# A fused attention and SwiGLU kernel: two weight loads ahead of a transposed load, an offset for every operation in the order, and warm-up on a constant

## The chip, the cores and the metric

The kernel runs on one core of a Trainium2 chip. The time is that of one execution on the device in microseconds (us); three runs of the kernel before gave 235.48, 235.54 and 235.83 us, so the median is 235.54 us.

A core has four compute engines that run side by side, each working through its own instructions in the order in which the program lists them: TensorE (PE in the profile, with its weight loads as PEld), VectorE (DVE), ScalarE (ACT) and GpSimd (POOL). SyncE (SP) issues most of the DMA transfers; its queue is SPq. An instruction that waits holds up everything behind it on its engine.

## The reference

The inputs are bfloat16: x is 2048 x 512, wqkv 512 x 1536, wo 512 x 512, w1 and w3 512 x 1376, w2 1376 x 512, gate_w has 512 entries.

```python
qkv = x @ wqkv                      # 32 heads of 16
scores = q @ k.T * 16 ** -0.5       # per head
mask = (i - j >= 0) & (i - j < 256) # causal, a window of 256 keys
a = softmax(where(mask, scores, -1e9)) @ v   # then heads joined, @ wo
b = (silu(x @ w1) * (x @ w3)) @ w2
g = sigmoid((x * gate_w).sum(-1))
out = g * a + (1 - g) * b
```

B_x is not used: both halves read A_x.

## The kernel before

**Layout.** x is held transposed in SBUF as `xT`, in four quarters of 512 tokens, called x0 to x3 here. x0 is loaded plainly and turned by TensorE (L383). x1, x2 and x3 are turned by the DMA, four transfers of 128 columns each (`turn_x`, issued by SP at L289). Attention goes by four chunks `c` of 128 columns (8 heads) and 16 key blocks `t` of 128 tokens. The SwiGLU half goes by four token blocks `tcb` of 512 and eleven column tiles `f` of 128, the last of them of 96 columns.

**Work on TensorE.** K and Q projections (L443), four matmuls of 512 columns each per chunk and quarter; V (L496), for two chunks at once; scores of a key block, 8 matmuls on 32-row strips (L551), and of the block edges, 32 small ones (L601); probabilities times V (`pv`, L691), in two halves per chunk and quarter, on 17-column strips; w1 and w3 (L841), the leftover columns (L778), w2 (L894), wo (L923) and the last tile's w2 in three parts (L950). The program calls the three shapes "full", "row" (L551, L601) and "column" (L691).

**Other engines.** ACT does the exponentials (L555, L605, 1.88 us each), half of the copies of K and the tanh of the SwiGLU half. POOL masks the exponentials (L560, L565, L618), rearranges V (L532) and copies the last columns of w1 and w3 into `wA` and `wB` (L754). DVE evacuates most of PSUM. Scores have one PSUM buffer of four banks (`su`), everything else has four of one bank (`ch`).

**The order.** `opening()` issues the first loads in a fixed order. Everything else is an `Op` handed to `Plan.add` with an engine, a duration, dependencies and a due time. `Plan.emit` is a list scheduler that runs in Python when the program is built: again and again it takes the engine that can start first, and on it, among the operations that can start at that moment, the one with the smallest due time, ties by number (`rank`). The result is a fixed order of instructions for each engine; on the chip they wait only for semaphores. The scheduler's idea of when a load has landed is a table, `landed`, in us.

Two constants in `rank` act on the shapes: while TensorE is in a shape other than full, row and column operations get due times smaller by `ADJ`; while it is in full shape, column operations get `SEP` added, which is negative. An exponential may be held back for up to `HOLD` ahead of other work on ACT.

**Numbers of operations.** Each `Op` has a running number, `len(self.ops)` at its creation. Number 17 is POOL's small write that gates x3: `late(25.8, ...)` makes an entry that ends at 25.8 us, a two-element memset on POOL with due time 25.8 that depends on it (L358), and four `turn_x` operations on SP behind it. The program thus uses POOL's place in its order to hold SP back. The rest of wqkv is gated in the same way near 67 us.

**SP's opening order.** x0's first half, K's weights (one half, the other by ACT), Q's weights, w1 and w3 columns 0:256, V's weights, x1 (four), w1 and w3 columns 256:768, x2 (one), w1 columns 768:1376, x2 (one), w3 columns 768:1376, x2 (two). Below, "first", "second" and "third columns" mean 0:256, 256:768 and 768:1376.

**Warm-up.** 25 matmuls on a tile `warm`, which DVE sets to zero (L312), run on TensorE from the start; two more stand before the first projection.

Of the kernel before, what the change touches and what calls it, by code (L numbers as in the profile page):

```python
# [8 lines left out]
ACT = mybir.ActivationFunctionType  # L9
BF16 = mybir.dt.bfloat16  # L10
# [5 lines left out]
P = 128  # L16
KB = 64
BIG = 3.0e38
SLACK = 0.04


PIPE = {"DVE": 0.105, "ACT": 0.112, "POOL": 0.045}
LAT = {"PE": 0.205}
# [23 lines left out]
class Plan:  # L47
# [7 lines left out]
    def add(self, eng, dur, fn, deps=(), due=0.0, take=(), free=(), lat=None, form="full", port=False):  # L55
        if lat is None:
            lat = LAT.get(eng, 0.05)
        op = Op(eng, dur, fn, deps, due, list(take), list(free), lat, len(self.ops), form, port)
        self.ops.append(op)
        return op  # L60
# [91 lines left out]
def kernel(  # L152
# [12 lines left out]
    nc = tc.nc  # L165
# [19 lines left out]
    SCALE = float(DH) ** -0.5  # L185
    WARM = 25

# [4 lines left out]
    xs = pp.tile([P, 4, D], BF16, name="xs")  # L192
    warm = pp.tile([P, P], BF16, name="warm")
    wqkv_sb = pp.tile([P, NDC, 3 * D], BF16, name="wqkv_sb")
# [38 lines left out]

    K = {"T0": 3.834, "TA": 174.183, "TF0": -2.174, "TF1": 214.702, "PV": -18.741, "EDGE": -2.057, "HOLD": -5.699, "LEAD": -2.792, "QLEAD": -4.754, "V": 6.656, "O0": 12.623, "O1": 1.536, "O2": 8.341, "O3": 35.5, "FE": 0.655, "PE": 7.925, "VE": -2.0, "MK": 33.193, "UP": 8.561, "_km": 1.0, "_lo": 1.0, "LE": 0.445, "ADJ": 6.464, "SEP": -25.111, "BE": 6.303, "OE": 5.748, "END": 6.616}
    plan = Plan({"su": 1, "ch": 4, "Em": len(Em), "Ee": len(Ee), "tt": 2, "h1": 2,
# [71 lines left out]
    def warm_up(n):  # L307
        for i in range(n):
            nc.tensor.matmul(su[:, 0, 0:P], lhsT=warm[:], rhs=warm[:], start=True, stop=True)

    def opening():
        nc.vector.memset(warm[:], 0.0)  # L312
        constants()
        warm_up(WARM)

        nc.scalar.activation(out=gt[:, 0:4], in_=warm[:, 0:4], func=ACT.Tanh)
        load_x(0, 2, nc.sync)
# [6 lines left out]
        load_w(wqkv_sb, A_wqkv, 2 * D, 2 * D + 2 * P)  # L324
        turn_x(1)
        load_w(w1_sb, B_w1, 2 * P, 6 * P)
        load_w(w3_sb, B_w3, 2 * P, 6 * P)
        turn_x(2, 0, 1)
        load_w(w1_sb, B_w1, 6 * P, F)
        turn_x(2, 1, 2)  # L330
        load_w(w3_sb, B_w3, 6 * P, F)
        turn_x(2, 2, 4)
# [9 lines left out]
    step = TA / (NDC * NT)  # L342
    landed = {"x": [3.75, 3.75, 4.45, 4.45, 12.2, 21.5], "w13": [7.2, 8.1, 15.4, 18.7],
              "qkv": [5.25, 6.2, 8.8], "gw": 8.0}

# [23 lines left out]

    x_in.append(late(25.8, xT[0:1, 0, 3 * 512:3 * 512 + 2], [lambda c=c: turn_x(3, c, c + 1) for c in range(NDC)], 1.27, 2.5))  # L370
    for b, us in ((1, 66.5), (0, 68.5), (2, 70.5)):
# [208 lines left out]
    def edge_batch(c, h):  # L580
# [56 lines left out]
        if K["_lo"]:  # L637
            edge_ready[(c, h)] = [add("POOL", 1.2, lambda lo=lo: low(lo), [x], due) for lo in (0, KB)]
            edge_ready[(c, h)].append(add("DVE", 0.45 if not last else 0.6, high, [x], due - K["MK"], port=True))
        else:  # L640
            edge_ready[(c, h)] = [add("DVE", 0.84, lambda half=half: mask(half), [x], due - K["MK"], port=True) for half in range(2)]
# [109 lines left out]
    for dst, c0, src in ((wA, 0, w1_sb[:, :, F0:F0 + FA]), (wA, FA, w3_sb[:, :, F0:F0 + FA]),  # L751
# [3 lines left out]

        w_ab.append(add("POOL", 0.4, w_copy, [w13_in[3]], 22.0))

# [6 lines left out]
    for tcb in range(NTC):  # L764
# [66 lines left out]
        for f in range(NFC):  # L831
# [33 lines left out]
            win = [w13_in[0 if f < 2 else 2 if f < 6 else 3]]  # L865
            win3 = [w13_in[1]] if f < 2 else []
            a = plan.pieces(HALF, 0.2155, lambda lo, hi, half=half, job=job: half(job, w1_sb, lo, hi),
# [134 lines left out]
```

## Time and profile before

| | |
|---|---|
| median of three runs | 235.54 us |
| the profiled execution | 236.38 us |
| its span, first to last instruction | 234.7 us |
| TensorE busy | 225.7 us (96%) |
| ScalarE busy | 182.8 us (78%) |
| VectorE busy | 179.5 us (77%) |
| GpSimd busy | 153.6 us (65%) |
| SP queue, share of the 16 DMA engines | 18.1% |

The profile is of one execution, whose own time is 236.38 us; 1.7 us of that lie outside the span. Matmuls are pipelined, so a group of matmuls overlaps the next one's start by some 0.16 us, and starts, not ends, tell the pace. A few per cent of the matmul records are missing. A timeline merges equal instructions: "x8" with a start and a duration is eight of them. The chain of waits is followed back from the last instruction; a line in it is a piece that held up the end.

### The profile page before, as it was taken

How to read it: one execution, taken by the hardware profiler on the slowest of the kernel's cores; microseconds unless marked ns; L12 is line 12 of the kernel's file. 1: busy time of each engine (PE TensorE's matmuls, PEld its weight loads, DVE VectorE, ACT ScalarE, POOL GpSimd, SP SyncE). 2: the span in 40 equal slices, each digit the busy share in tenths (PEclk: the TensorE clock that was granted, in tenths of full speed). 3: DMA queues.
4: the chain of work that ended last, by engine and by line, in shares of the span. 5: the costliest groups of instructions: out<-in, count | busy, mean ns of one | idle time of the engine just before them, and what ended most of it. 6: DMA issues, size and time to landing. Idle time of an engine off the chain costs nothing.

```text
span 234.7 us, 8251 instructions
## 1 busy us (share of the span) xinstructions
PE 225.7 (96%) x3590; PEld 116.1 (49%) x3626; DVE 179.5 (77%) x318; ACT 182.8 (78%) x165; POOL 153.6 (65%) x245
## 2 busy tenths in 40 slices
PE   8899999999999999999999999999999999999995
PEld 7454644555454444446464556435444445445553
DVE  5455985973789897988297988969498978869675
ACT  3488998976779899887889999988778997887310
POOL 7164979579765986565668768697669855474500
PEclk9999999999999999999999999999999999999999
DMA  6999034600004000000000002200000002120102
GB/s 191 193 210 291 4 45 108 189 20 1 3 19 120 3 8 17 3 3 3 0 4 3 3 4 62 53 3 4 0 3 3 3 6 56 58 91 6 67 25 89
DMA packets 20652, 11.57 MB, mean 49 GB/s; under 512 B 10024, under 2 KB 20616, under 8 KB 20616
## 3 DMA queue, kind: packets, MB, share of 16 engines
q1 hardware_dynamic: 19920, 10.62, 18.1%
q8 instruction: 28, 0.46, 0.9%
q10 hardware_dynamic: 696, 0.43, 0.6%
q14 instruction: 8, 0.07, 0.1%
HBM read 6.85 MB, written 2.10 MB: 38 GB/s over the span
## 4 chain that ended last, share of the span: by engine, by line
PE 80%; SPq 6%; DMA 6%; POOL 4%; issue 2%; DVE 1%
PE ch L841 26%; PE ch L894 15%; PE ch L443 10%; PE ch L691 8%; PE su L551 7%; PE ch L923 6%; SPq L289 5%; PE ch L496 4%; DMA wqkv_sb<-in_A_wqkv_dram 2%; DMA w_sb<-in_B_w_dram 2%; PE su L601 2%; SPq L296 1%; DMA xT<-in_A_x_dram 1%; POOL Ee L618 1%; PE ch L950 1%
## 5 line engine op out<-in xcount | busy, mean ns | idle before, releaser
L555 ACT ACTIVATE Em<-su 128x2048 bf16<-128x2048 f32 x60 | 112.6, 1877 | 24.8 <-PE su L551 20.8
L841 PE MATMUL ch<-xT,w_sb 128*128 128x512 bf16 x301 | 76.3, 380 | 1.6 <-issue 0.8
L560 POOL TENSOR_SCALAR_AFFINE_SELECT Em<-Em 64x512 bf16<-64x512 bf16 x60 | 43.4, 724 | 36.5 <-ACT Em L555 35.6
L618 POOL TENSOR_SCALAR_AFFINE_SELECT Ee<-Ee 64x1024 bf16<-64x1024 bf16 x32 | 37.6, 1174 | 16.3 <-ACT Ee L605 15.0
L841 PEld LDWEIGHTS <-w_sb 128*128 128x128 bf16 x320 | 28.4, 98 | 34.4 <-issue 4.9
L565 POOL TENSOR_SCALAR_AFFINE_SELECT Em<-Em 64x512 bf16<-64x512 bf16 x56 | 37.3, 667 | 3.3
L855 DVE SCALAR_TENSOR_TENSOR h<-tt,ch 128x512 bf16<-128x512 bf16 (+1 forms) x44 | 29.8, 678 | 11.1 <-ACT tt L851 10.7
L894 PE MATMUL ch<-w_sb,hT 128*128 128x512 bf16 x141 | 36.1, 380 | 1.0 <-issue 0.8
L443 PE MATMUL ch<-xT,wqkv_sb 128*128 128x512 bf16 (+1 forms) x131 | 34.1, 369 | 1.8 <-DMA wqkv_sb<-in_A_wqkv_dram 0.9
L532 POOL COPY vs<-vs 64x256 bf16<-64x256 bf16 x64 | 28.9, 452 | 7.3 <-DVE vs L520 2.7
L605 ACT ACTIVATE Ee<-su 128x2048 bf16<-128x2048 f32 x16 | 30.0, 1878 | 4.2 <-PE su L601 3.1
L861 DVE SCALAR_TENSOR_TENSOR hT<-h,ch 128x512 bf16<-128x512 bf16 x40 | 27.2, 679 | 2.5 <-PE ch L841 1.0
L851 ACT ACTIVATE tt<-ch 128x512 bf16<-128x512 f32 (+1 forms) x44 | 26.2, 595 | 1.3 <-PE ch L841 1.1
L691 PEld LDWEIGHTS <-vs 128*17 128x17 bf16 x1664 | 20.6, 92 | 6.2 <-issue 4.6
L691 PE MATMUL ch<-Em,vs 128*17 128x256 bf16 (+2 forms) x672 | 22.7, 242 | 0.1
L691 PE MATMUL ch<-Ee,vs 128*17 128x64 bf16 x992 | 22.3, 193 | 0.0
L894 PEld LDWEIGHTS <-hT 128*128 128x128 bf16 x150 | 13.5, 98 | 16.2 <-issue 2.7
L898 DVE TENSOR_SCALAR bsb<-ch,omg 128x512 bf16<-128x512 f32 x15 | 11.0, 738 | 11.6 <-PE ch L894 11.4
L443 PEld LDWEIGHTS <-wqkv_sb 128*128 128x128 bf16 x136 | 12.4, 99 | 14.2 <-issue 2.1
L551 PE MATMUL su<-qT,kz 32*128 32x256 bf16 x240 | 17.3, 278 | 0.1
L496 PE MATMUL ch<-wqkv_sb,xT 128*128 128x256 bf16 x128 | 16.7, 273 | 0.2 <-DVE tn L715 0.2
L551 PE MATMUL su<-qT,k 32*128 32x256 bf16 x240 | 16.7, 268 | 0.0
(84 smaller groups left out, 245.9 us busy)
## 6 DMA issues: line engine op xcount, KB each, us to landing
out_dram<-ot SPq DMA_DIRECT2D x15, 128.0 KB, 1.7
wqkv_sb<-in_A_wqkv_dram SPq DMA_DIRECT2D x5, 256.0 KB, 4.9
w_sb<-in_B_w_dram SPq DMA_DIRECT2D x2, 608.0 KB, 5.5
w_sb<-in_B_w_dram SPq DMA_DIRECT2D x3, 384.0 KB, 3.8
w_sb<-in_B_w_dram SPq DMA_DIRECT2D x2, 512.0 KB, 5.2
w_sb<-in_B_w_dram SPq DMA_DIRECT2D x2, 256.0 KB, 6.3
wo_sb<-in_A_wo_dram SPq DMA_DIRECT2D x4, 128.0 KB, 2.3
xs<-in_A_x_dram SPq DMA_DIRECT2D x1, 256.0 KB, 2.8
```

Of the source, the lines that this page charges most:

```text
L443: nc.tensor.matmul(pst[:, t0:t1], lhsT=wqkv_sb[:, dc, col + c * P:col + (c + 1) * P], rhs=xT[:, dc, tq * 512 + t0:tq * 512 + t1], start=(d ...
L532: nc.gpsimd.tensor_copy(out=v_of(to, base, a), in_=v_of(half, 0, a))
L551: nc.tensor.matmul(su[:, s, a * 256:(a + 1) * 256], lhsT=head_keys(r, t, a), rhs=qT[r, q0:q0 + 256], start=True, stop=True)
L555: nc.scalar.activation(out=Em[job.at["Em"]][:], in_=su[:].rearrange("p s (a q) -> p s a q", a=2), func=ACT.Exp, scale=SCALE)
L560: nc.gpsimd.affine_select(out=e, in_=e, pattern=[[0, 8], [1, KB]], compare_op=ALU.is_ge, fill=0.0, base=0, channel_multiplier=-1)
L565: nc.gpsimd.affine_select(out=e, in_=e, pattern=[[0, 8], [-1, KB]], compare_op=ALU.is_ge, fill=0.0, base=-1, channel_multiplier=1)
L605: nc.scalar.activation(out=Ee[ej.at["Ee"]][:].rearrange("p s t k q -> p s (t k q)"), in_=su[:], func=ACT.Exp, scale=SCALE)
L618: nc.gpsimd.affine_select(out=e, in_=e, pattern=[[0, 4], [0, 4], [1, KB]], compare_op=ALU.is_ge, fill=0.0, base=0, channel_multiplier=-1)
L691: nc.tensor.matmul(po[32 * s:32 * s + VW, lo - 512 * w:hi - 512 * w], lhsT=vs[:, i, a * VW:(a + 1) * VW], rhs=mov, start=(n == 0), stop=(n ...
L841: nc.tensor.matmul(ch[job.at["ch"]][:], lhsT=wA[:, dc, :] if joint else w[:, dc, f * P:(f + 1) * P], rhs=xT[:, dc, tcb * 512:(tcb + 1) * 512],
L855: nc.vector.scalar_tensor_tensor(out=h1[job.at["h1"]][ru, :], in0=tt[job.at["tt"]][rg, :], scalar=1.0, in1=ch[job.at["ch"]][rg, :], op0=AL ...
L894: nc.tensor.matmul(bps[:], lhsT=ht[:, mm * P:(mm + 1) * P], rhs=w2_sb[0:fs, f, :], start=(f == 0), stop=(f == NFC - 1))
```

## The change

- In `opening()`, the second columns of w1 and w3 are issued ahead of x1, the third columns of w1 ahead of x2, and those of w3 after the first of x2's four transfers.
- `landed` has new times. Up to now w1's and w3's second columns had one entry for both, and so had their third columns; now each load has its own.
- The gate of x3 is entered at 20.5 us, not 25.8.
- `Plan.add` adds `SHIFT[n]` to the due time of operation n. The list has 1520 numbers with a spread (standard deviation) of 15.2. Number 17 is 16.41.
- The constants in `K` are new, among them the spacing of the attention's due times (`TA`), `ADJ` and `SEP`; some durations in the scheduler's tables differ.
- The warm-up is 26 matmuls on a constant of ones that the program has anyway; the tile `warm` and its memset go.

```diff
+SHIFT = [
+    0, 0, 0, 0, 0, 0, 0, 0, 0, 0, 0, 0, 0, 0, 0, 0, 0, 16.41, 17.18, -1.15, 9.76, -3.89, -4.94, -3.98, -10.53, 6.23,
...
+    7.93, 89.38, 4.39, -2.31, 9.54, 0, 105.24, -33.46, -30.49, -22.75, -41.96,
+]
-PIPE = {"DVE": 0.105, "ACT": 0.112, "POOL": 0.045}
+PIPE = {"DVE": 0.105, "ACT": 0.112, "POOL": 0.0}
@@ def add
-        op = Op(eng, dur, fn, deps, due, list(take), list(free), lat, len(self.ops), form, port)
+        n = len(self.ops)
+        due += SHIFT[n] if n < len(SHIFT) else 0.0
+        op = Op(eng, dur, fn, deps, due, list(take), list(free), lat, n, form, port)
@@
-    WARM = 25
+    WARM = 26
-    warm = pp.tile([P, P], BF16, name="warm")
-    K = {"T0": 3.834, "TA": 174.183, "TF0": -2.174, "TF1": 214.702, "PV": -18.741, "EDGE": -2.057, "HOLD": -5.699, "LEAD": -2.792, "QLEAD": -4.754, "V": 6.656, "O0": 12.623, "O1": 1.536, "O2": 8.341, "O3": 35.5, "FE": 0.655, "PE": 7.925, "VE": -2.0, "MK": 33.193, "UP": 8.561, "_km": 1.0, "_lo": 1.0, "LE": 0.445, "ADJ": 6.464, "SEP": -25.111, "BE": 6.303, "OE": 5.748, "END": 6.616}
+    K = {"T0": 3.896, "TA": 206.496, "TF0": 0.258, "TF1": 224.823, "PV": -10.571, "EDGE": -3.579, "HOLD": -5.698, "LEAD": -3.708, "QLEAD": -6.04, "V": 10.539, "O0": 15.639, "O1": -7.5, "O2": 2.592, "O3": 31.747, "FE": 1.561, "PE": 14.011, "VE": -7.01, "MK": 68.425, "UP": 9.802, "_km": 1.0, "_lo": 1.0, "LE": -2.888, "ADJ": 16.608, "SEP": -51.372, "BE": 8.744, "OE": 1.749, "END": 5.976}
@@ def warm_up
-            nc.tensor.matmul(su[:, 0, 0:P], lhsT=warm[:], rhs=warm[:], start=True, stop=True)
+            ones = nc.const_aps.tensor_like(1.0, ident[:])
+            nc.tensor.matmul(su[:, 0, 0:P], lhsT=ones, rhs=ones, start=True, stop=True)
@@ def opening
-        nc.vector.memset(warm[:], 0.0)
-        nc.scalar.activation(out=gt[:, 0:4], in_=warm[:, 0:4], func=ACT.Tanh)
+        nc.scalar.activation(out=gt[:, 0:4], in_=nc.const_aps.tensor_like(1.0, gt[:, 0:4]), func=ACT.Tanh)
         load_w(wqkv_sb, A_wqkv, 2 * D, 2 * D + 2 * P)
-        turn_x(1)
         load_w(w1_sb, B_w1, 2 * P, 6 * P)
         load_w(w3_sb, B_w3, 2 * P, 6 * P)
+        turn_x(1)
+        load_w(w1_sb, B_w1, 6 * P, F)
         turn_x(2, 0, 1)
-        load_w(w1_sb, B_w1, 6 * P, F)
+        load_w(w3_sb, B_w3, 6 * P, F)
         turn_x(2, 1, 2)
-        load_w(w3_sb, B_w3, 6 * P, F)
         turn_x(2, 2, 4)
@@
-    landed = {"x": [3.75, 3.75, 4.45, 4.45, 12.2, 21.5], "w13": [7.2, 8.1, 15.4, 18.7],
-              "qkv": [5.25, 6.2, 8.8], "gw": 8.0}
+    landed = {"x": [3.6, 3.6, 4.4, 4.4, 14.5, 20.6], "w13": [7.45, 8.3, 10.8, 16.6, 12.2, 18.8],
+              "qkv": [5.25, 6.5, 9.0], "gw": 8.0}
@@
-    x_in.append(late(25.8, xT[0:1, 0, 3 * 512:3 * 512 + 2], [lambda c=c: turn_x(3, c, c + 1) for c in range(NDC)], 1.27, 2.5))
+    x_in.append(late(20.5, xT[0:1, 0, 3 * 512:3 * 512 + 2], [lambda c=c: turn_x(3, c, c + 1) for c in range(NDC)], 1.27, 2.5))
@@ def edge_batch
-            edge_ready[(c, h)] = [add("POOL", 1.2, lambda lo=lo: low(lo), [x], due) for lo in (0, KB)]
-            edge_ready[(c, h)].append(add("DVE", 0.45 if not last else 0.6, high, [x], due - K["MK"], port=True))
+            edge_ready[(c, h)] = [add("POOL", 1.15, lambda lo=lo: low(lo), [x], due) for lo in (0, KB)]
+            edge_ready[(c, h)].append(add("DVE", 0.6, high, [x], due - K["MK"], port=True))
@@
-        w_ab.append(add("POOL", 0.4, w_copy, [w13_in[3]], 22.0))
+        w_ab.append(add("POOL", 0.4, w_copy, [w13_in[5]], 22.0))
@@
-            win3 = [w13_in[1]] if f < 2 else []
+            win3 = [w13_in[1 if f < 2 else 4 if f < 6 else 5]]
```

86 rows, old and new, of the table SHIFT are left out of this document.

## The prediction

> **What bounds the kernel now.** First the page's busy times and its chain that ended last, then TensorE's waits, then the timeline of TensorE at the places of those waits, then the chain for the start.
>
> ```profile
> PE 225.7 (96%) x3590; PEld 116.1 (49%) x3626; DVE 179.5 (77%) x318; ACT 182.8 (78%) x165; POOL 153.6 (65%) x245
> PE 80%; SPq 6%; DMA 6%; POOL 4%; issue 2%; DVE 1%
> ```
>
> TensorE is the bound: no other engine is above 78%, and the chain runs on it for 80% of the span. From its waits:
>
> ```profile
> PE ch L443 <- DMA wqkv_sb<-in_A_wqkv_dram: 0.9, 1, 0.9
> PE ch L443 <- DMA xT<-in_A_x_dram: 0.4, 1, 0.4
> ```
>
> Two waits for loads; all other rows of that view are 0.2 us pieces. Those are missing records: TensorE has 36 gaps of 0.21 to 0.23 us, one matmul of 512 columns long, and the groups lack 36 such records (w1/w3 316 of 336, w2 156 of 165, projections 115 of 120, wo 62 of 64). What is left are two places, in TensorE's timeline:
>
> ```profile
> 17.70 0.38 PE L443 MATMUL ch<-xT,wqkv_sb 128*128 128x512 bf16 x1
> 18.20 0.82 PE L841 MATMUL ch<-xT,w_sb 128*128 128x512 bf16 x3
> ...
> 37.45 0.81 PE L443 MATMUL ch<-xT,wqkv_sb 128*128 128x512 bf16 x3
> 38.62 0.38 PE L443 MATMUL ch<-xT,wqkv_sb 128*128 128x512 bf16 x1 [0.36 <-DMA xT<-in_A_x_dram]
> ...
> 73.78 1.46 PE L841 MATMUL ch<-xT,w_sb 128*128 128x512 bf16 x6
> 75.17 0.29 PE L551 MATMUL su<-qT,kz 32*128 32x256 bf16 x4
> 75.29 0.28 PE L551 MATMUL su<-qT,k 32*128 32x256 bf16 x4
> 75.50 1.25 PE L841 MATMUL ch<-xT,w_sb 128*128 128x512 bf16 x5
> ```
>
> Starts of 512-column matmuls stand 0.2155 us apart. From 17.70 to 18.20 is 0.28 too long: w3's second columns, for which the weight load at 18.19 waits. From 37.45 three matmuls reach to 38.10, the fourth starts at 38.62: 0.52 us for x3. The last four lines show a change of shape: six matmuls from 73.78 end at 75.07 and the row starts at 75.17, 0.10 later; its second half starts at 75.29, streams 0.11 and is followed at 75.50, again 0.10 later. **From 8.8 us to the last matmul TensorE thus stands still for 0.80 us in all; the rest is matmuls and changes of shape.** The start, in the chain that ended last:
>
> ```profile
> 1.83 5.85 DMA wqkv_sb<-in_A_wqkv_dram
> 7.70 1.16 SPq L289
> 8.90 1.26 SPq L289
> 10.21 1.26 SPq L289
> ...
> 17.11 5.54 DMA w_sb<-in_B_w_dram
> 22.70 0.40 POOL wA L754
> ...
> 31.43 0.10 POOL xT L358
> 31.55 1.12 SPq L289
> ...
> 35.88 2.70 DMA xT<-in_A_x_dram
> 38.62 0.38 PE ch L443
> ```
>
> The second transfer of x1 was issued 0.02 us after Q's weights had landed (7.68), with which it has nothing to do: the second DMA behind V's load waits for the one that carried Q, whatever it loads. And x3 is late because POOL waited until 22.70 for w3's third columns, then worked without a pause and came to the gate at 31.43, planned for 25.8 or later.
>
> **The change, part by part.** The sum is made against the profiled execution, 236.38 us, span 234.7; the median of 235.54 is 0.84 lower. The profiled execution has a wait of 1.0 us for Q's weights (K's eight matmuls start 0.11 apart to 6.57, Q's start at 7.73). I take that to be most of the 0.84 and subtract the changes from both alike.
>
> *Second columns first.* w1's takes the place of x1's first transfer (issued at 4.93), w3's that of the second (7.70). Both were issued at 11.51 and 13.03 and seen by TensorE at 16.73 and 18.19, 5.2 later. By 5.2 they land near 10.1 and 12.9. The wait of 0.28 goes: -0.28 (bounds -0.28 and 0).
>
> *x1 behind them.* Four more instructions now stand behind that second place on SP's queue. w3's issue lasts 0.51, then four transfers at 1.30 (8.90 to 10.21): 8.25, 9.55, 10.85 and 12.15, the last landing 2.7 to 3.9 later (the shortest and the median of the twelve), at 14.9 to 16.1. Before, Q's projection of x1 ran at 14.03. Other work covers this: 4 groups of the first columns at 0.86, V's 16 matmuls at 0.11, two rows at 0.43 and the gate's turn at 0.3 make 6.4 us, which lasts from 8.8 to 15.2, and the second columns are 8 groups more, 6.9 us, to 22. Only the fixed order can put the projection too early. In before it was planned for 12.2 or later and ran at 14.03, 1.8 behind; with 14.5 and the same lag it comes at 16.3, after the landing. *x2*: third columns and x2 follow from 13.5; with 1.48 us (11.51) for the first plain load after transposes, or 0.58 (14.87), x2's last transfer is issued at 18.9 to 19.8 against 18.96 before and lands at 21.6 to 23.7; planned 20.6 plus the lag makes 22.4. For both together +0.2, near the row of before, where this lag left no wait; bounds 0 and 1.3.
>
> *x3 sooner.* The gate may go from 20.5, but number 17's offset of 16.41 makes its due time 36.9, so POOL takes it only when nothing more urgent can start. w3's third columns are issued near 16 to 17, against 17.11, so POOL's wait for them shrinks by at most 1. In before x3 landed 5.2 after its plan (25.8, four at 1.27 and 2.5 make 33.4; 38.58), of which the lag of 1.8 hides a part. Of 5.2 less 1.8, 3.4, TensorE saw 0.52, so the order left 2.9 of room. I take the wait of 0.52 as gone: -0.52; bounds -0.52 (none) and +2.9 (a wait of 3.4, no room left). Nothing else waits on SP there.
>
> *Warm-up.* No wait for DVE's memset: TensorE can start near 0.8 (ACT's first work is at 0.81) instead of 1.07, and 26 matmuls at 0.107 end at 3.6, against 3.71 when the turning of x0 started. x0 was issued at 0.82 and landed 2.8 later, 3.62. At most -0.09, and none of it survives the wait for Q's weights; 0, bounds -0.1 and +0.1. ACT's table load hides the missing memset.
>
> *Order.* There are 76 rows and 16 pairs of column halves, each pair in one piece, 15 of them next to a row, which saves one change of 0.10. A row needs the exponential before it (1.88 plus two handovers, 2.4 from row to row), and a pair takes 1.5, so no pair can have rows on both sides without a wait: one more change, 0.1, is all that is to be gained. To lose: a split pair costs two changes, 0.20. Among the list's entries for the pairs only chunk 1, quarter 2 has its second half much later than its first (-37.59 and -3.74; the next is 13.8), and `ADJ` of 16.6 works against a split. 0; bounds -0.1 and +0.6 (two splits, two neighbours lost). The middle has no wait to remove. The end does not change: the last matmul is at 231.7, the last evacuation at 231.94, and some 2.7 us of store follow; 0, bounds -0.2 and +0.3.
>
> Sum: -0.28 + 0.2 - 0.52 = -0.6. From 236.38 this gives 235.8, from the median **234.9 us**.
>
> **The rivals.** (1) *Hidden anyway.* The gains were waits of the profiled execution; with Q's weights sooner the loads may have been in time, or the new order may spend the 0.6 at x1 or x2 (bound +1.3). For it: the median is lower than the profile. Against: TensorE would be earlier too, so the waits stay. Time 235.5. (2) *x3 comes later for the order than now (the slower one).* Place: the fourth matmul of Q's projection of x3. The plan has x3 5.3 us sooner, so it may place this projection sooner; if POOL again reaches the gate some 5 us behind its plan, TensorE waits. Price: with half the room of now a wait of 3.4 - 1.45 = 1.95, and 235.54 - 0.28 + 0.2 - 0.52 + 1.95 = 236.9. It decides once the wait is over 1.07 (236.01 less 234.94). For it: the offset of 16.41. Against: the plan knows POOL's other work, and w3's third columns are less late. (3) *Torn shapes.* Seven split pairs at 0.20 or as many lost neighbours: +1.4, so 236.3. For it: offsets of 15 against an `ADJ` of 16.6. Against: the entries of the pairs. (4) *The clock doubles sooner.* 128-column matmuls run 0.107 apart to 5.4, and 256 columns take 0.11 from 6.1 on, so the clock doubled near 6.0 us. If an earlier start brought that before 3.7, 16 transposes would take 0.85 less; K's weights (issued by ACT at 1.50, landing 3.8 later, 5.3) let K start 0.33 sooner, so at most -0.3: 234.6. The Trainium skill, "TensorE: Matmul & The Clock Gate", Part 1, says that the clock is released after one busy window of about 3.4 us and that the windows run freely; by that rule 0.2 us can be worth a whole window or nothing. The trace shows one doubling and cannot tell which.
>
> **How the numbers follow.** A change under 0.2%, 0.47 us, can hardly be told from none here: the bounds are 235.07 and 236.01. Forecast 0.54, with its own range 234.6 to 235.2, of which 0.46 lies below 235.07; (4) 0.04; (1) 0.19; (2) 0.13; (3) 0.10. Faster 0.50, same 0.27, slower 0.23. The range: 234.5, the forecast with the -0.1s and the clock's part, to 236.4, which leaves out the worse halves of (2) and (3), some 0.12, and 0.04 below.
>
> **What would show it.** Right: no TensorE wait for w1/w3 or `xT`; x1's first transfer issued right behind w3's second columns near 8.2; the gate of x3 on POOL before 31; 16 unbroken column pairs. Wrong: a DMA wait on L443 over 0.6 us, pairs in two pieces, waits of TensorE on ACT or DVE in the middle, or a last matmul later than 231.7.

## The result and the profile after

The changed kernel takes 237.42 us (four executions, 236.98 to 237.92); the kernel before takes 235.62 us beside it (235.48 to 235.83). The ratio is 1.0082, with a 95% interval of 1.0059 to 1.0105: it is slower by 0.8%, where 234.9 us was forecast and the range ended at 236.4.

The profiled execution of the changed kernel took 236.98 us, 0.60 more than that of before. It splits into three pieces:

| | before | after | difference |
|---|---|---|---|
| first matmul of w1 starts (us) | 8.83 | 7.58 | -1.25 |
| from there to the last matmul: "the body" | 222.86 | 224.70 | +1.84 |
| last matmul to the end of the execution | 4.69 | 4.70 | +0.01 |

The first piece varies from execution to execution with the landing of Q's weights: over the profiles below it ends between 7.16 and 8.83 us, also for kernels whose opening is the same. The body is the part that the kernel's order decides, but for waits for loads, which differ between executions: with before's order and loads they are 0.80 us in the profile of before, 0.27 in warm_alone and 1.8 in before_no_min below. Its +1.84 is close to the 1.80 between the medians. From here on each kernel is told by its time (a median) and its body (one profile each). (Kernels whose plan puts a matmul or two of a projection ahead of that first w1 matmul have a body shorter by up to 0.2 for it.)

All lines of kernel.py stand about 92 further down: w1 and w3 are L933, the projections L535, the column halves L783, VectorE's two products of the SwiGLU half L947 and L953, GpSimd's masks of the edges L710 and VectorE's L716 and L720.

The busy times and the shares of the chain that ended last, from the page of the changed kernel:

```profile
PE 225.5 (96%) x3588; PEld 115.3 (49%) x3627; DVE 183.3 (78%) x317; ACT 182.4 (78%) x165; POOL 154.6 (66%) x245
PE 83%; DVE 9%; ACT 4%; issue 2%; DMA 1%; DVEq 0%
```

TensorE is busy as long as before. In the chain, SP's queue and GpSimd have gone and the DMAs are down from 6% to 1%, as the forecast wanted, and VectorE has come up from 1% to 9%. TensorE's waits (us in total, times, longest) name it:

```profile
PE ch L933 <- DVE h L947: 1.0, 1, 1.0
...
PE ch L535 <- DVE qT L574: 0.6, 1, 0.6
PE ch L475 <- DMA xs<-in_A_x_dram: 0.3, 1, 0.3
PE ch L783 <- DVE hT L953: 0.3, 1, 0.3
...
PE ch L535 <- DVE h L947: 0.2, 1, 0.2
```

No row is left for w1, w3 or `xT`. Where starts of matmuls stand further apart than their sizes and changes of shape explain, TensorE stands still for 0.39 us at 21.0, 0.29 at 65.1, 0.39 at 123.5, 0.07 at 130.6, 1.20 at 131.6 and 0.62 at 172.0: 2.96 us in the middle of the kernel, all of it for VectorE, where before had 0.80, all of it for loads. With two changes of shape more (171 against 169, 0.2 us) that is 2.4 us; the body shows 1.84, and of the difference up to 0.2 is the matmul moved ahead of it. Some 0.3 is not accounted for.

The largest of the stalls, in the timeline of the changed kernel (start, duration; lines of GpSimd, VectorE and TensorE from one stretch):

```profile
129.44 2.36 POOL L710 TENSOR_SCALAR_AFFINE_SELECT Ee<-Ee 64x1024 bf16<-64x1024 bf16 x2
...
129.86 0.75 DVE L883 TENSOR_SCALAR gq<-gt 128x4 f32<-128x4 f32 x1
129.97 1.99 PE L933 MATMUL ch<-xT,w_sb 128*128 128x512 bf16 x8
...
130.78 1.55 DVE L716 TENSOR_TENSOR Ee<-Ee,medge 128x1024 bf16<-128x1024 bf16 x1
132.26 0.68 DVE L947 SCALAR_TENSOR_TENSOR h<-tt,ch 128x512 bf16<-128x512 bf16 x1
132.99 0.81 PE L933 MATMUL ch<-xT,w_sb 128*128 128x512 bf16 x3 [1.04 <-DVE h L947]
```

Read it from below. TensorE waits for `h`, the product that empties a bank of `ch`. That product comes some 1.5 us late, behind two operations of VectorE that take longer here than they do undisturbed, both beside GpSimd's masks of L710. The minimum on L716, VectorE's mask of the edges, takes 1.55 us instead of 0.69, while GpSimd masks other columns of the same tile `Ee`: 0.86 late. And `gq`, an operation on four columns, takes 0.75 instead of 0.16: 0.59 late.

### The profile page after: what moved, and what is told of

Its sections match the earlier page's. It is cut to its first block, busy times and chain, and to the rows that moved or that the text cites. A ratio compares the mean times of both kernels' runs of the same rounds, so it can differ in the third digit from the quotient of the medians.

```text
span 235.3 us, 8251 instructions
## 1 busy us (share of the span) xinstructions
PE 225.5 (96%) x3588; PEld 115.3 (49%) x3627; DVE 183.3 (78%) x317; ACT 182.4 (78%) x165; POOL 154.6 (66%) x245
## 4 chain that ended last, share of the span: by engine, by line
PE 83%; DVE 9%; ACT 4%; issue 2%; DMA 1%; DVEq 0%
PE ch L933 27%; PE ch L986 15%; PE ch L535 10%; PE ch L783 9%; PE su L643 7%; PE ch L1015 6%; PE ch L588 4%; ACT Ee L697 2%; PE su L693 2%; DVE Ee L716 2%; DVE Ee L720 2%; DMA xs<-in_A_x_dram 1%; PE ch L1042 1%; DVE h L947 1%; ACT Em L647 1%
## 5 line engine op out<-in xcount | busy, mean ns | idle before, releaser
L933 PE MATMUL ch<-xT,w_sb 128*128 128x512 bf16 x302 | 76.7, 380 | 2.4 <-DVE h L947 1.0
L657 POOL TENSOR_SCALAR_AFFINE_SELECT Em<-Em 64x512 bf16<-64x512 bf16 x56 | 38.4, 686 | 30.5 <-ACT Em L647 28.5
L652 POOL TENSOR_SCALAR_AFFINE_SELECT Em<-Em 64x512 bf16<-64x512 bf16 x60 | 41.0, 684 | 14.0 <-ACT Em L647 11.7
L710 POOL TENSOR_SCALAR_AFFINE_SELECT Ee<-Ee 64x1024 bf16<-64x1024 bf16 x32 | 40.4, 1261 | 11.1 <-ACT Ee L697 9.8
L933 PEld LDWEIGHTS <-w_sb 128*128 128x128 bf16 x320 | 28.6, 98 | 35.9 <-issue 6.8
L947 DVE SCALAR_TENSOR_TENSOR h<-tt,ch 128x512 bf16<-128x512 bf16 (+1 forms) x44 | 29.6, 675 | 8.4 <-ACT tt L943 8.3
L624 POOL COPY vs<-vs 64x256 bf16<-64x256 bf16 x64 | 28.2, 441 | 11.5 <-DVE vs L598 5.5
L535 PE MATMUL ch<-xT,wqkv_sb 128*128 128x512 bf16 (+1 forms) x126 | 33.1, 366 | 1.7 <-DVE qT L574 0.6
L953 DVE SCALAR_TENSOR_TENSOR hT<-h,ch 128x512 bf16<-128x512 bf16 x40 | 26.8, 672 | 1.5
L783 PEld LDWEIGHTS <-vs 128*17 128x17 bf16 x1664 | 20.6, 92 | 6.3 <-issue 5.0
L783 PE MATMUL ch<-Em,vs 128*17 128x256 bf16 (+2 forms) x672 | 22.6, 242 | 0.3 <-DVE hT L953 0.3
L783 PE MATMUL ch<-Ee,vs 128*17 128x64 bf16 x992 | 22.1, 193 | 0.0
L986 PEld LDWEIGHTS <-hT 128*128 128x128 bf16 x150 | 13.5, 98 | 15.2 <-issue 1.5
L535 PEld LDWEIGHTS <-wqkv_sb 128*128 128x128 bf16 x136 | 12.5, 97 | 14.4 <-issue 4.4
```

The costliest lines, as they stand in the source:

```text
L535: nc.tensor.matmul(pst[:, t0:t1], lhsT=wqkv_sb[:, dc, col + c * P:col + (c + 1) * P], rhs=xT[:, dc, tq * 512 + t0:tq * 512 + t1], start=(d ...
L624: nc.gpsimd.tensor_copy(out=v_of(to, base, a), in_=v_of(half, 0, a))
L652: nc.gpsimd.affine_select(out=e, in_=e, pattern=[[0, 8], [1, KB]], compare_op=ALU.is_ge, fill=0.0, base=0, channel_multiplier=-1)
L657: nc.gpsimd.affine_select(out=e, in_=e, pattern=[[0, 8], [-1, KB]], compare_op=ALU.is_ge, fill=0.0, base=-1, channel_multiplier=1)
L710: nc.gpsimd.affine_select(out=e, in_=e, pattern=[[0, 4], [0, 4], [1, KB]], compare_op=ALU.is_ge, fill=0.0, base=0, channel_multiplier=-1)
L783: nc.tensor.matmul(po[32 * s:32 * s + VW, lo - 512 * w:hi - 512 * w], lhsT=vs[:, i, a * VW:(a + 1) * VW], rhs=mov, start=(n == 0), stop=(n ...
```

## The experiments

Every ratio is against the kernel before on the same chip.

| run | time, us | ratio [95%] | body, us | waits of TensorE in the body |
|---|---|---|---|---|
| changed kernel | 237.42 | 1.0082 [1.0059, 1.0105] | 224.70 | 2.96, VectorE |
| warm_alone | 236.04 | 1.0008 [0.9980, 1.0037] | 222.47 | 0.27, x3 |
| sequence_only | 236.24 | 1.0019 [0.9991, 1.0047] | 223.52 | 1.5, x1 |
| table_only | 242.00 | 1.0277 [1.0232, 1.0321] | 227.32 | 4.6, VectorE and ACT |
| loads_alone | 240.68 | 1.0215 [1.0171, 1.0259] | 227.30 | 4.6, VectorE and ACT |
| loads_and_warm | 240.88 | 1.0227 [1.0189, 1.0266] | 227.32 | as loads_alone |
| no_offsets | 237.21 | 1.0059 [1.0035, 1.0083] | 224.33 | 2.1, mostly VectorE |
| changed_old_sequence | 239.32 | 1.0125 [1.0079, 1.0171] | 226.74 | 1.9 for w1, then as changed |
| changed_no_min | 234.87 | 0.9959 [0.9941, 0.9977] | 222.11 | 0.29 |
| before_no_min | 235.51 | 0.9999 [0.9975, 1.0024] | 224.14 | 1.8, loads |
| changed_no_gpsimd_mask | 234.48 | 0.9934 [0.9909, 0.9959] | 221.84 | none on VectorE |
| before_min_twice | 243.23 | 1.0293 [1.0266, 1.0320] | 230.62 | mostly VectorE |
| before_x3_early | 235.28 | 0.9972 [0.9950, 0.9995] | 222.05 | none for loads |
| changed_in_order | 235.11 | 0.9972 [0.9947, 0.9998] | 222.14 | none on VectorE |
| no_offsets_in_order | 236.10 | 1.0015 [0.9992, 1.0038] | 223.00 | 1.1 |

### The change in pieces

**loads_alone** is before with the new sequence of loads, the new table, the gate of x3 at 20.5 and w3's dependencies; constants, offsets and warm-up stay. Its diff is that of two runs below, sequence_only and table_only, together.

> The kernel before with the new sequence of loads, the new table of landing times and x3's gate at 20.5 us; no offsets, old constants, old warm-up. Theory A (the offsets make an order in which TensorE waits for VectorE; the loads are good): 235.0 us, 0.2 to 1.0 below the kernel before, no wait of TensorE on w1, w3 or xT. Theory B (the load sequence itself costs): 236.5 or more, with a DMA wait on a projection of x1 or x2.

It took 240.68 us, 5 us more than before, with no wait for any load, so neither theory holds as it stands. TensorE's waits in it:

```profile
PE ch L841 <- DVE h L855: 0.8, 1, 0.8
PE su L551 <- ACT Em L555: 0.5, 1, 0.5
PE ch L443 <- DVE h L855: 0.5, 1, 0.5
PE ch L894 <- ACT k L466: 0.4, 1, 0.4
```

They lie at 21, 26, 51, 161, 163, 183, 194 and 232 us, far from the loads that were moved, and there are 177 changes of shape. A list scheduler takes a new table as a new problem: an entry of 20 us can change the order at 190. So the loads can't be judged by a kernel that plans anew for them with constants that were set for the old table.

**warm_alone** has the constant warm-up and nothing else.

```diff
-    WARM = 25
+    WARM = 26
...
-            nc.tensor.matmul(su[:, 0, 0:P], lhsT=warm[:], rhs=warm[:], start=True, stop=True)
+            ones = nc.const_aps.tensor_like(1.0, ident[:])
+            nc.tensor.matmul(su[:, 0, 0:P], lhsT=ones, rhs=ones, start=True, stop=True)
...
-        nc.vector.memset(warm[:], 0.0)
...
-        nc.scalar.activation(out=gt[:, 0:4], in_=warm[:, 0:4], func=ACT.Tanh)
+        nc.scalar.activation(out=gt[:, 0:4], in_=nc.const_aps.tensor_like(1.0, gt[:, 0:4]), func=ACT.Tanh)
```

> The kernel before with the warm-up of 26 matmuls on the constant and nothing else. Theory A: within 0.3 us of the kernel before, 235.3 to 235.7. Theory C (the warm-up shifts the moment at which TensorE's clock doubles, and the change's loss or its spread of 0.9 us sits there): more than 0.5 us away, or runs that differ by 0.7 us or more.

236.04 us, ratio 1.0008, and the interval of 0.9980 to 1.0037 shows no difference. Its executions spread over 1.7 us, but those of before beside it spread over 2.8, so the spread says nothing for theory C. **loads_and_warm** puts the edits of the two together.

> The kernel before with the new loads and the new warm-up together, no offsets and old constants. Theory A: the sum of the two alone, 234.8 us, the fastest of the four. Theory B: as the loads alone, 236.5 or more.

240.88 us, body 227.32 against 227.30 without the warm-up: the parts don't act on each other.

**sequence_only** issues the loads in the new sequence under before's own order of instructions; **table_only** has the new table and the order that follows from it, with the loads issued as before.

The first has this diff:

```diff
-        turn_x(1)
         load_w(w1_sb, B_w1, 2 * P, 6 * P)
         load_w(w3_sb, B_w3, 2 * P, 6 * P)
+        turn_x(1)
+        load_w(w1_sb, B_w1, 6 * P, F)
         turn_x(2, 0, 1)
-        load_w(w1_sb, B_w1, 6 * P, F)
+        load_w(w3_sb, B_w3, 6 * P, F)
         turn_x(2, 1, 2)
-        load_w(w3_sb, B_w3, 6 * P, F)
```

and the second the rest:

```diff
-    landed = {"x": [3.75, 3.75, 4.45, 4.45, 12.2, 21.5], "w13": [7.2, 8.1, 15.4, 18.7],
-              "qkv": [5.25, 6.2, 8.8], "gw": 8.0}
+    landed = {"x": [3.6, 3.6, 4.4, 4.4, 14.5, 20.6], "w13": [7.45, 8.3, 10.8, 16.6, 12.2, 18.8],
+              "qkv": [5.25, 6.5, 9.0], "gw": 8.0}
...
-    x_in.append(late(25.8, xT[0:1, 0, 3 * 512:3 * 512 + 2], [lambda c=c: turn_x(3, c, c + 1) for c in range(NDC)], 1.27, 2.5))
+    x_in.append(late(20.5, xT[0:1, 0, 3 * 512:3 * 512 + 2], [lambda c=c: turn_x(3, c, c + 1) for c in range(NDC)], 1.27, 2.5))
...
-        w_ab.append(add("POOL", 0.4, w_copy, [w13_in[3]], 22.0))
+        w_ab.append(add("POOL", 0.4, w_copy, [w13_in[5]], 22.0))
...
-            win3 = [w13_in[1]] if f < 2 else []
+            win3 = [w13_in[1 if f < 2 else 4 if f < 6 else 5]]
```

> The kernel before with SP's opening loads in the new sequence and nothing else: table of landing times, gate of x3, constants, so every compute engine's order, are those of before. New theory D (the loads themselves do no harm; the loss of the loads alone came from the order that the scheduler made out of the new table): from the first w1 matmul to the last matmul 222.6 us or less (222.9 in the profile of before, 227.3 with loads alone), time within 0.6 of the kernel before, no wait on w1 or w3. Theory B (the transfers): 226 or more for that stretch, with DMA waits.

> The kernel before with the new table, the gate entry of 20.5 us and the dependencies on w3's own entries, while the loads are issued in the old sequence. Theory D: the order of the loads alone, so some 4 us of waits of TensorE on VectorE far from the loads remain, 240 or more. Theory B: the loss goes away with the sequence, 236 or less.

They part the two halves of loads_alone. The table alone costs what loads_alone costs (body 227.32 and 227.30; its median is longer by 1.3 us, which its one profile does not explain). The sequence alone takes away the waits for w3 and x3 and brings one for x1, because before's order wants Q's projection of x1 at 13.1; TensorE's timeline of sequence_only:

```profile
13.13 0.38 PE L443 MATMUL ch<-xT,wqkv_sb 128*128 128x512 bf16 x1
14.31 1.36 PE L443 MATMUL ch<-xT,wqkv_sb 128*128 128x512 bf16 x3 [0.80 <-DMA xT<-in_A_x_dram]
```

Three gaps here add up to 1.5 us, so the body is 0.9 longer than expected. The loads behind the second columns need an order made for them.

**changed_old_sequence** is the reverse: the changed kernel with its order, its loads issued in the old sequence.

```diff
+        turn_x(1)
         load_w(w1_sb, B_w1, 2 * P, 6 * P)
         load_w(w3_sb, B_w3, 2 * P, 6 * P)
-        turn_x(1)
-        load_w(w1_sb, B_w1, 6 * P, F)
         turn_x(2, 0, 1)
-        load_w(w3_sb, B_w3, 6 * P, F)
+        load_w(w1_sb, B_w1, 6 * P, F)
         turn_x(2, 1, 2)
+        load_w(w3_sb, B_w3, 6 * P, F)
```

> The changed kernel with SP's opening loads issued in the old sequence; the plan, and so every engine's order, is the changed one. Theory D: the waits on VectorE stay (2.5 to 3 us), and in addition TensorE waits for second columns that the plan expects at 10.8 and 12.2 and that come at 16.7 and 18.2: 238 to 241. Theory B: the loss goes, 236 or less.

239.32 us, 2.04 of body more than the changed kernel, of which one row holds nearly all:

```profile
PE ch L933 <- DMA w_sb<-in_B_w_dram: 1.8, 1, 1.8
```

So in the changed kernel the new sequence is worth 2 us of body (between the ratios it is 1 us, with intervals that overlap), and the loss of 0.8% is not there.

**no_offsets** is the changed kernel with an empty list of offsets.

```diff
-SHIFT = [
...
-]
+SHIFT = []
```

> The changed kernel with an empty list of offsets: new constants, new loads, new warm-up. Theory A: the waits of TensorE on VectorE in the middle go, 235.0 us. Rival A2 (the new constants, made for the offsets or not, carry the loss): 237 or more, with the same waits.

237.21 us, body 224.33 against 224.70. The new constants by themselves have already taken back 3 of the 4.5 us of body that the table costs, and VectorE is already waited for:

```profile
PE su L554 <- DVE qT L485: 1.2, 1, 1.2
```

The offsets as such are neither the gain nor the loss.

**before_x3_early** takes the late x3 alone out of the kernel before: its transfers are issued behind x2's, without the gate, and the plan is told the old times, so that the order stays.

```diff
         turn_x(2, 2, 4)
+        turn_x(3)
...
-    x_in.append(late(25.8, xT[0:1, 0, 3 * 512:3 * 512 + 2], [lambda c=c: turn_x(3, c, c + 1) for c in range(NDC)], 1.27, 2.5))
+    prev = add("POOL", 0.08, lambda: None, [arrive(25.8)], 25.8)
+    for c in range(NDC):
+        prev = add("SP", 1.27, lambda: None, [prev], 25.8 - 30.0, lat=0.0)
+    x_in.append(add("DMA%d" % len(plan.ops), 0.0, lambda: None, [prev], 25.8, lat=2.5))
```

> The kernel before with x3's four transfers issued right behind x2's in the opening; the gate's memset and its four places in SP's order are kept in the plan but do nothing, so every other engine's order is that of before. If x3's wait is worth what the prediction took (0.52 in the profile of before): no DMA wait near 37, time 0.3 to 0.8 below the kernel before. If the transfers get in the way of others: no gain.

235.28 us, ratio 0.9972, body 222.05 against 222.86, and no wait for a load is left. Of these 0.80, 0.52 is x3's wait. The other 0.28 is w3's, which this edit doesn't touch: in this execution, as in warm_alone, SP issued the second columns at 10.0 to 10.4 instead of 11.51, since Q's weights had landed sooner (6.17 and 6.37 us, 7.68 in before), and w3 came in time.

### The minimum

The stalls of the changed kernel, but for the one of 0.07, follow a minimum of VectorE (L716, L720) that stands beside a mask of GpSimd (L710), so each of the two was taken away.

**changed_no_min** and **before_no_min** leave out VectorE's minimum (the first diff), **changed_no_gpsimd_mask** leaves out GpSimd's half of the masks of `Ee` (the second).

```diff
         def high():
-            full = 2 if last else 4
-            e = Ee[ej.at["Ee"]][:, :, 0:full, 1, :]
-            nc.vector.tensor_tensor(out=e, in0=e, in1=medge[:, 1][:, None, None, :].to_broadcast([P, 4, full, KB]),
-                                    op=ALU.min)
...
+            pass
```

```diff
         def low(lo):
-            e = Ee[ej.at["Ee"]][lo:lo + KB, :, :, 0, :]
-            nc.gpsimd.affine_select(out=e, in_=e, pattern=[[0, 4], [0, 4], [1, KB]], compare_op=ALU.is_ge, fill=0.0,
-                                    base=0, channel_multiplier=-1)
+            pass
```

> The changed kernel without VectorE's masking of the far edge blocks (the minimum with a mask, on the lines of high()), so its output has unmasked edges; the order of all other instructions is unchanged. Theory E (the waits of TensorE come from VectorE's minimum, slowed to 1.4 to 1.7 us when GpSimd masks the same tile at the same time): the waits of 0.4, 0.3, 0.4, 1.2 and 0.6 us go, at most 0.5 us of them left, and the stretch from the first w1 matmul to the last matmul falls from 224.7 to 222.3. Rival F (the order is too tight whatever VectorE's speed): 2 us of waits or more remain.

> The kernel before without the same masking, its output likewise with unmasked edges. Theory E: no wait of TensorE to remove in the middle, so the stretch stays within 0.4 of 222.9 us and the time within 0.5 of the kernel before. If it gains 2 us as well, the minimum is simply in the way in both kernels and E does not explain the difference.

> The changed kernel with VectorE's minimum left in and GpSimd's masking of the near edge blocks left out (the two selects of low(), so its output has those unmasked). Theory E1 (the minimum is late because GpSimd works beside it): the minimum takes 0.4 to 0.7 us throughout, at most 0.6 us of the waits of TensorE on VectorE remain, the stretch from the first w1 matmul to the last is 222.4. Rival E2 (the minimum is too much work for this order even at its own speed): 1.5 us or more of waits remain and the stretch is above 223.5.

Without the minimum the changed kernel takes 234.87 us: 2.55 less, and 0.4% faster than before. The kernel before gains nothing (0.9999). Its body is longer than expected, 224.14, for the loads: the first matmul of w1 came at 7.16 in this execution and TensorE waited 1.8 for the second columns and x3. Less the waits, it is 222.3, against 222.1 in before. The 0.29 left in changed_no_min comes behind a four-column operation (`omg`) that takes 1.14 beside a mask, instead of 0.16. Without GpSimd's mask the changed kernel takes 234.48 us though VectorE still does all of its minima, and these are now short. Groups of VectorE by form in the changed kernel (count, total, mean ns of one, idle time before):

```profile
L716 DVE TENSOR_TENSOR Ee<-Ee,medge 128x1024 bf16<-128x1024 bf16 x12 | 10.8, 902 | 1.5 <-ACT Ee L697 1.4
...
L720 DVE TENSOR_TENSOR Ee<-Ee,mlast 128x512 bf16<-128x512 bf16 x4 | 4.5, 1128 | 0.0
```

and in changed_no_gpsimd_mask:

```profile
L714 DVE TENSOR_TENSOR Ee<-Ee,medge 128x1024 bf16<-128x1024 bf16 x12 | 8.6, 720 | 1.3 <-ACT Ee L697 1.1
...
L718 DVE TENSOR_TENSOR Ee<-Ee,mlast 128x512 bf16<-128x512 bf16 x4 | 1.9, 470 | 0.0
```

So it is not the minimum's own work that costs, but VectorE's work and the mask at the same time.

**before_min_twice** asks whether before has room on VectorE: it does each minimum twice.

```diff
-        def high():
+        def high_once():
...
+        def high():
+            high_once()
+            high_once()
```

> The kernel before with VectorE's minimum done twice in a row (the second changes nothing), so each is 0.4 to 1.4 us longer, at the same place in the order. If the order of before has room for a late VectorE (theory E with room): the stretch grows by less than 1 us from 222.9, the time by less than 1. If it has no more room than the changed one and is only spared by where its minima fall: waits of 2 us or more, 238 or above.

243.23 us, body 7.8 longer, with waits on VectorE through the whole kernel:

```profile
PE ch L695 <- DVE h L859: 1.8, 3, 0.8
...
PE ch L695 <- DVE qT L482: 0.8, 1, 0.8
```

The expectation of room fell. The 20 minima take 14.3 us in before and the 40 of this kernel 32.2; of these 18 us TensorE felt 7.8. A VectorE that is 77% busy took in more than half of the extra work, but had no room at the places where it empties a bank that TensorE wants next. So it is not room everywhere that spares before. That it is where its slow minima fall is the reading that is left; no run moves them.

### The order enforced

The plan has a rule on this: operations of GpSimd and those of VectorE flagged `port` take turns in its reckoning, as if they shared one place (they may overlap by 0.045 us). On the chip nothing holds them to it, since the minimum and the masks work on different columns and wait for the same exponential only. In before's plan all 16 minima come behind both masks of their tile; in the changed one twelve come ahead of one or both. On the chip both engines are then released by the same exponential. The minimum shown above at 130.78, for one, stands between the two masks in the plan, and on the chip it came 0.13 us after the second had started.

It is not `MK` that puts them there, though it sets a minimum's due time 68.4 us ahead instead of 33.2. `Plan.emit` is Python and can be run without the chip: with 33.193 in the changed kernel it still puts twelve ahead. It is `PIPE["POOL"]`, which the diff lowers from 0.045 to 0. The plan opens the shared place 0.045 us before an operation ends (`port = est + op.dur - 0.045`) and has GpSimd itself free `PIPE["POOL"]` before that end. With 0.045 a waiting mask can start at the same instant as a minimum, and the plan takes the mask; with 0 a minimum that is ready goes in first. Changing this number alone in before puts 11 minima ahead. In no_offsets 14 are ahead, so it isn't the offsets, and with 0.045 put back there none is. These are counts of the plan; no run on the chip has this number alone.

**changed_in_order** makes the chip keep to the plan: behind each of these twelve minima (the expectation below says 11) VectorE copies one column of the part that the later mask will write, so the mask has to wait.

```diff
+    seen = pp.tile([P, 1], BF16, name="seen")
...
+        left = [0, KB]
...
         def low(lo):
+            left.remove(lo)
...
+            if left:
+                r = slice(left[0], left[-1] + 1)
+                nc.vector.tensor_copy(out=seen[r, :], in_=Ee[ej.at["Ee"]][r, 0, 0, 0, 0:1])
```

> The changed kernel with one tiny copy on VectorE behind each minimum that the plan puts ahead of GpSimd's selects on the same tile (11 of 16); the copy reads an element that the select will write, so the select waits for the minimum as in the plan. All work is kept. Theory E1 (the two run side by side on the chip, one after the other in the plan): the minima behind which the select waits take 0.4 to 0.7 us, the waits of TensorE on VectorE fall from 3 us to under 0.8, the stretch from the first w1 matmul to the last is 222.5, the time 234.9, below the kernel before. Rival E3 (leaving out work is what helped, the order does not matter): the waits stay above 2 us.

235.11 us over twelve executions, ratio 0.9972 with an interval of 0.9947 to 0.9998: faster than the changed kernel by some 2.3 us and than before by 0.3%. The body is 222.14. At the second of the changed kernel's stalls, near 65 us, the changed kernel had this (VectorE and GpSimd):

```profile
63.23 0.43 DVE L716 TENSOR_TENSOR Ee<-Ee,medge 128x512 bf16<-128x512 bf16 x1 [0.47 <-ACT Ee L697]
63.28 1.39 POOL L710 TENSOR_SCALAR_AFFINE_SELECT Ee<-Ee 64x1024 bf16<-64x1024 bf16 x1
63.57 1.37 DVE L720 TENSOR_TENSOR Ee<-Ee,mlast 128x512 bf16<-128x512 bf16 x1
64.86 0.68 DVE L947 SCALAR_TENSOR_TENSOR h<-tt,ch 128x512 bf16<-128x512 bf16 x1
```

and changed_in_order this:

```profile
63.78 0.42 DVE L720 TENSOR_TENSOR Ee<-Ee,medge 128x512 bf16<-128x512 bf16 x1 [0.48 <-ACT Ee L698]
64.13 0.42 DVE L724 TENSOR_TENSOR Ee<-Ee,mlast 128x512 bf16<-128x512 bf16 x1
64.46 0.14 DVE L728 COPY seen<-Ee 65x1 bf16<-65x1 bf16 x1
...
64.74 1.15 POOL L714 TENSOR_SCALAR_AFFINE_SELECT Ee<-Ee 64x1024 bf16<-64x1024 bf16 x1 [0.98 <-DVE seen L728]
```

The minimum for the last block goes from 1.37 to 0.42 us. The mask waits 0.98 us, and nobody waits long for it: in TensorE's waits only a row of 0.2 names it. Its rows in this kernel:

```profile
PE ch L476 <- DMA xs<-in_A_x_dram: 0.6, 1, 0.6
PE ch L790 <- POOL Ee L714: 0.2, 1, 0.2
```

Twelve added copies of 0.14 us on the engine that TensorE waits for, and the kernel is faster: here, which of the two engines waits is worth more than 1.7 us of work.

**no_offsets_in_order** has the copies of changed_in_order and the empty list of no_offsets.

> The same copy in the changed kernel with an empty list of offsets (new constants, loads and warm-up). If the offsets are worth something once the plan holds: slower than the changed kernel with the copy by 0.3 us or more. If the constants carry all of it: equal within 0.3, and below 236. Waits of TensorE on VectorE under 1.2 us in either case.

236.10 us, body 223.00. With the order kept, the offsets are worth 0.86 of body (222.14), and about 1 us of time; without it they were worth nothing (224.70 with them, 224.33 without). In these two pairs fine shifts of the plan pay only where the chip keeps nearer to what the plan reckoned.

## Why the prediction was wrong, point by point

- **Second columns first (-0.28).** Right in that the wait is gone: SP issues them at 5.06, in x1's old place, and TensorE doesn't wait for them. But the 0.28 was a wait of that execution of before: warm_alone and before_x3_early, with before's loads there, have none, and before_no_min has 0.58. SP's timeline after:

```profile
5.06 1.71 SPq L388 DMA_DIRECT2D w_sb<-in_B_w_dram  x2
6.81 5.12 SPq L381 DMA_TRANSPOSE xT<-in_A_x_dram  x4
```

- **x1 and x2 behind them (+0.2, 0 to +1.3).** It was the lower end, 0. x1's first transfer went out at 6.81, 1.4 us sooner than worked out, because Q's weights landed sooner, at 6.38 us. The profile of before, with 7.68, is the odd one: in all others they land at 6.2 to 7.0. That the new order covers x1 and the old one doesn't is shown by sequence_only: 1.5 us, a little above the upper end.
- **x3 sooner (-0.52).** Right. GpSimd comes to the gate at 24.30, not at 31.43, and the wait is gone. before_x3_early has this term alone and gains 0.7 us between the medians (its interval reaches from 0.1 to 1.2); 0.52 of its gain in body is this wait.

```profile
24.30 0.09 POOL L450 MEMSET xT<- 1x2 bf16 x1
```

- **Warm-up (0, -0.1 to +0.1).** Right in time (1.0008), and Q's weights hide the start as it said; but x0 comes later and not sooner, which is told below, with what was not expected.
- **End (0).** Right: 4.70 us after the last matmul, 4.69 before.
- **Order (0, bounds -0.1 and +0.6).** This is the step that failed, with its sentence "The middle has no wait to remove". It counted what the order could do to the shapes of TensorE, and there it was nearly right: two changes of shape more, one torn pair. It took for granted that VectorE and GpSimd would go on having their work done in time, and priced nothing for a new order between these two. In its place came 2.96 us of waits on VectorE, where the bound allowed 0.6. changed_no_min, changed_no_gpsimd_mask and changed_in_order each take them away in another way, and end at 234.87, 234.48 and 235.11 us, about where the forecast stood.

The sum without that step held: changed_in_order is 0.55 us under the kernel before, forecast 0.6. As a set of terms this is no proof, since x3 alone gives as much.

The trace of before had the signs of it, and the prediction didn't look. Groups of before by form, and one place in its timelines:

```profile
L624 DVE TENSOR_TENSOR Ee<-Ee,medge 128x1024 bf16<-128x1024 bf16 x12 | 10.2, 850 | 0.0
...
L628 DVE TENSOR_TENSOR Ee<-Ee,mlast 128x512 bf16<-128x512 bf16 x4 | 2.1, 528 | 0.0
```

```profile
23.53 1.15 POOL L618 TENSOR_SCALAR_AFFINE_SELECT Ee<-Ee 64x1024 bf16<-64x1024 bf16 x1
...
23.96 1.25 DVE L624 TENSOR_TENSOR Ee<-Ee,medge 128x1024 bf16<-128x1024 bf16 x1
```

A mean of 850 ns where single ones take 0.69 says that some take far longer, and 23.96 shows why. Six of before's 20 minima are held by more than 0.2 us, some 2.7 us over all 20, and TensorE feels none of it. The changed kernel also has six, but some 5.5 us over all, and a copy that is held by 0.96; five of the six stand ahead of a product or a copy that frees a bank which TensorE wants next. The thing to ask about was the diff's `PIPE`: what the plan does where GpSimd and VectorE meet.

**The rivals.** (2) didn't happen: the waits went. Nor did (1) in the changed kernel, but it had a point: with Q's weights sooner w3's wait was gone in two kernels without any change of its load. (3) named the order as the danger and torn shapes as its price of 1.4; 0.2 of that came. A rival by which the order makes VectorE late was not among them, though "waits of TensorE on ACT or DVE in the middle, or a last matmul later than 231.7" stood among the signs of a wrong prediction; both are what the trace shows. (4) came and went: in the changed kernel's profile 128-column matmuls start 0.056 us apart from 4.2 us on, so the clock had doubled by then (near 6.0 before); in that of changed_in_order, with the same opening, they stay 0.107 apart to 5.8. The Trainium skill, "TensorE: Matmul & The Clock Gate", Part 1, on windows that run freely, agrees with a doubling that the kernel doesn't place. It decides nothing: what follows waits for Q's weights.

**What stays open.** That `PIPE` is what put the minima in the way is read from the plan; no run has it alone, and any edit of it gives a new order throughout, not only for the minima. Whether before would gain from keeping the chip to its plan wasn't run either. Why the new table under the old constants waits at just those eight places wasn't followed up.

## What to carry to other kernels

Where a planner fixes the order of each engine, an edit of its inputs changes all of the order, and its price has to be looked for on every engine that frees the bottleneck's buffers, not at the edit alone. If the planner keeps two engines apart because they share something, look whether a dependency makes the chip do the same; if not, compare the mean and the largest duration of those operations in the trace, and add the cheapest dependency there is. An engine of 77% busy time can have no slack at the places where the bottleneck waits for it, and which instruction is held back there can be worth more than the work itself.

## What was not expected of the hardware

**VectorE and GpSimd take turns, whole instructions long.** A minimum of two tiles in SBUF that starts while a GpSimd mask or copy runs doesn't run slower; it waits for the end of that instruction and then needs nearly its usual time. One of 1024 columns ends 0.54 us behind the other's end, one of 512 columns 0.27, within 0.02 in the pairs of before, the changed kernel and changed_in_order, but for one of 0.61. In the changed kernel, the second of the masks shown above at 129.44:

```profile
130.65 1.15 POOL L710 TENSOR_SCALAR_AFFINE_SELECT Ee<-Ee 64x1024 bf16<-64x1024 bf16 x1
```

It ends at 131.80, and the minimum that started at 130.78 ends at 132.33, 0.53 later. In before, 23.53 + 1.15 = 24.68 and 23.96 + 1.25 = 25.21, again 0.53. It holds the other way round too: the mask that starts at 63.28 in the changed kernel beside the minimum of 63.23 takes 1.39 instead of 1.15, and masks that start right behind the start of a minimum of 1024 columns take 1.60. A copy from SBUF to SBUF with one input is held as well:

```profile
170.95 1.24 DVE L561 COPY kz<-k 128x512 bf16<-128x512 bf16 x1
```

It takes 0.28 elsewhere, and here ends 0.15 us behind two masks (169.37 + 2.67 = 172.04). Size is no protection: the four-column `gq` shown at 129.86 takes 0.75 and ends with the first of the two masks, at 130.6. The product on L947 with one input in SBUF and one in PSUM is never held: it takes 0.68 beside a mask at 132.26 as without one, and 0.69 at most in the whole kernel. The Trainium skill, "SBUF — State Buffer", section "Who interferes with whom", says this: an operation of VectorE with two inputs in SBUF contends with a GpSimd instruction that reads SBUF, and so does one in a 2-port fast mode, which copies and operations with a scalar can enter; whichever is first keeps the shared ports for the whole instruction, and the other is blocked. The traces agree, with the numbers above. So a minimum and a mask released by the same exponential can cost VectorE most of the mask's 1.15 us when the mask gets in first (0.94 to 0.95 where one of 512 columns met it early, 1.04 at most), and the order of before could have been judged by it.

**The constant warm-up has x0 come later.** In the seven profiles with the zeroed tile the turning of x0 starts at 3.71 to 3.85 us, right behind the warm-up. In the nine with the constant it starts at 4.01 to 4.34, and waits for x0's load, which SP issues at 0.82 in both and which lands at 3.55 to 3.80 in the seven and at 3.96 to 4.29 in the nine. So the warm-up that starts 0.2 us sooner loses 0.3 to 0.6 at its end, which the wait for Q's weights hides again. In the nine, ACT, whose first `Tanh` no longer reads the zeroed tile, issues the load of x0's other half at 0.87, in the seven at 1.05; whether that delays the first half was not tested.
